# Attention on one core: a tile's six inverse row sums, turned by one transpose, spread over a head's partitions through DRAM, and multiplied on GpSimd

## The chip, the core and the metric

The kernel runs on one core of a Trainium2 chip. The metric is device time in microseconds (us) of one execution; lower is better. The engines are called by the short names of the profile: PE is TensorE (PEld its weight loads), DVE is VectorE, ACT is ScalarE, POOL is GpSimd, and SP is SyncE, which here issues the DMAs.

## The reference, cut to what matters

```
mask   = q_bucket[:, :, :, None] == k_bucket[:, :, None, :]     # hash of 6 sign bits
scores = np.where(mask, scale * q @ k.T, -1e9)
scores = scores - max(scores, axis=-1)
attn   = np.exp(scores)
attn   = attn / (np.sum(attn, axis=-1, keepdims=True) + 1e-9)
x      = attn @ v             # 2 x 8 heads, 768 x 768 scores, head size 64
x      -> [1536, 512] -> a gated MLP (silu) -> a second MLP with softmax and layer norm
```

The change touches one thing: the division of a head's output by its row sums.

## The kernel before, in words

Attention works on eight pairs of heads (a batch and two heads j = 0, 1). A pair's 768 query rows are cut into two halves n of 384 rows. A "quarter" h is one head of one half, three tiles of 128 query rows; there are 32 quarters, numbered in the order of the work, and the quarters with j = 1 close a half: `ends(h)` is true for them (h = 2, 3 and then every odd h from 5 to 31). The main loop (L819 to L868) runs one slot per tile of 128 query rows, 96 of them and nine to drain. In a slot `maxima` takes the row maxima on DVE (L563), `transposes` turns the exponentials of two slots ago on PE (L595, L597), `scores` makes the next tile's scores (four matmuls, L553), `highs` and `lows` split the turned tiles on ACT (L606) and DVE (L610), `values` multiplies by v for the quarter five slots back (L631 to L636), and `exps` is the exponential on ACT (L577). In many slots PE also turns four blocks of the next pair's q and k (L475) or makes hashes (L514). l is the number of a slot within a pair's twelve (slot modulo 12).

The output of a quarter comes off PE transposed: 128 partitions are the high and the low part of the 64 columns of v, and the 384 query rows run along a partition. `results(h)` (L671 to L720) is a generator whose steps the main loop calls in later slots. For a closing quarter: step 1 copies the product to `both_of` on ACT (L703), and two DMAs on SP (L704, L705) lay its halves beside those of the other head, so that `xf` and `low` hold both heads, 64 partitions each; step 2, a slot later, is `widen` (L649): `r`, the 6 inverse sums of each of 128 partitions (2 heads x 3 tiles, L645 and L646, DVE), is stretched to 128 x 384 by two multiplications on POOL (L654); step 3 adds `low` to `xf` on POOL (L710); step 4 is `spread` (L660): three PE transposes of 128 x 128 (L665) put the stretched sums into a PSUM bank; step 5 multiplies `xf` by that bank on DVE (L714); step 6 splits the product into `xh` and `xl` on POOL (L717, L720). Steps 4 and 5 fall into slots with l = 2 and l = 8, step 6 into the slot after. `both_of`, whose buffer has the tag "both", and the PSUM bank "pp" have one buffer each; "pp" also holds the turned blocks and the hashes of the next pair. The last two quarters take another way (L687 to L697).

The order of each engine's work in attention is written out by hand: an engine carries out its instructions in the order in which this loop emits them, and SP issues its DMAs in that order as well. `behind` makes POOL's instruction wait for the latest row maxima. Loads of the next pairs are emitted by `splitting` (L787), at l = 9 the one of q (384 KB). After attention come the two MLPs, on the same engines; their first matmuls (L1132) read `xh` and `xl`.

Of the kernel before, what the change touches and what calls it, by code (L numbers as in the profile page):

```python
# [10 lines left out]
F32 = mybir.dt.float32  # L11
# [10 lines left out]
P = 128  # L22
# [49 lines left out]
def hash_attention_then_two_mlps(  # L72
# [16 lines left out]
    nc = tc.nc  # L89
    B, H, S, D = q.shape  # L90
# [5 lines left out]
    HALF = S // 2  # L96
    CH = C // 2
# [20 lines left out]
    at = ctx.enter_context(ExitStack())  # L118
# [40 lines left out]
    idf = e_sides[2][0][:, :P]  # L159
    make_identity(nc, idf)  # L160
    nc.vector.tensor_copy(idr, idf)
    idf = idr.bitcast(F32)
# [25 lines left out]
    up, down, both = slice(0, D), slice(D, P), slice(0, P)  # L188
# [41 lines left out]
    with at:  # L230
        vp = at.enter_context(tc.tile_pool(name="vp", bufs=2))
        ab = at.enter_context(tc.tile_pool(name="ab", bufs=4))
        sm = at.enter_context(tc.tile_pool(name="sm", bufs=4))
        xs = at.enter_context(tc.tile_pool(name="xs", bufs=2))
        ps_s = at.enter_context(tc.tile_pool(name="ps_s", bufs=1, space=PSUM))
        ps_t = at.enter_context(tc.tile_pool(name="ps_t", bufs=2, space=PSUM))
        ps_a = at.enter_context(tc.tile_pool(name="ps_a", bufs=1, space=PSUM))
        ps_p = at.enter_context(tc.tile_pool(name="ps_p", bufs=1, space=PSUM))
# [56 lines left out]
        def behind(work):  # L295

            if bias_of:
                tc.add_manual_dep(
                    work.ins, bias_of[-1].ins.name,
                    mybir.DependencyInfo(  # L300
                        mybir.DependencyClass.Sync, mybir.DependencyReason.DATA
                    ),
                    reason="behind the maxima",
                )
# [193 lines left out]
        def hashes(p, n, apart=True):  # L498
# [30 lines left out]
        s_of, e_of, t_of, eh_of, el_of, av_of, total_of, r_of, rs_of, x_of = (  # L529
            {} for _ in range(10)  # L530
        )
        NQ = NSLOT // CH

        def quarter(h):


            p, l = divmod(h, 4)
            return (p, l // 2, l % 2) if p == 0 else (p, l % 2, l // 2)

        def ends(h):  # L540

            return quarter(h)[1] == 1
# [95 lines left out]
        def sums(h):  # L638
# [7 lines left out]
            nc.vector.reciprocal(r.rearrange("p j c -> p (j c)"), total)  # L646
            r_of[p, n] = r

        def widen(p, n, tag="wide"):  # L649

            r = r_of[p, n]
            wide = xs.tile([P, CH, 2, D], F32, tag=tag, name="wide", bufs=1)
            for j in range(2):
                behind(nc.gpsimd.tensor_mul(  # L654
                    wide[:, :, j, :], one.unsqueeze(2).to_broadcast([P, CH, D]),
                    r[:, j, :].unsqueeze(2).to_broadcast([P, CH, D]),
                ))
            r_of[p, n] = wide

        def spread(p, n):  # L660

            wide = r_of.pop((p, n))
            rs = ps_p.tile([P, 512], F32, tag="pp", name="pp")
            for c in range(CH):
                nc.tensor.transpose(  # L665
                    rs[:, c * P:(c + 1) * P],
                    wide[:, c].rearrange("p j d -> p (j d)"), idf,
                )
            rs_of[p, n] = rs[:, :HALF]

        def results(h):  # L671


            if not 0 <= h < NQ:
                return
            p, j, n = quarter(h)
            b, hp = pairs[p]
            at = slice(j * D, (j + 1) * D)
            av = av_of.pop(h)
            if j == 0:  # L680
                x_of[p, n] = [
                    xs.tile([P, HALF], F32, tag=tag, name=tag, bufs=bufs)
                    for tag, bufs in (("xf", 3), ("low", 2))
                ]
            xf, low = x_of[p, n]
            cols = slice(b * S + n * HALF, b * S + (n + 1) * HALF)
            if h >= NQ - 2:  # L687

                nc.scalar.copy(low[0:D], av[D:P])
                yield  # L690
                nc.vector.tensor_add(xf[at], av[0:D], low[0:D])
                if j == 0:
                    return
                ends_of["DVE"] = nc.vector.tensor_mul(xf, xf, rs_of.pop((p, n)))
                ends_of["ACT"] = nc.scalar.copy(xh[:, hp, cols], xf)
                nc.vector.tensor_sub(xl[:, hp, cols], xf, xh[:, hp, cols].bitcast(F32))
                return  # L697
            if j == 0:
                nc.scalar.copy(xf, av)
                nc.sync.dma_start(low[0:D], xf[D:P])  # L700
                return
            both_of = xs.tile([P, HALF], F32, tag="both", name="both", bufs=1)
            nc.scalar.copy(both_of, av)  # L703
            nc.sync.dma_start(low[D:P], both_of[D:P])  # L704
            nc.sync.dma_start(xf[D:P], both_of[0:D])  # L705
            del x_of[p, n]
            yield
            widen(p, n)
            yield
            behind(nc.gpsimd.tensor_add(xf, xf, low))  # L710
            yield
            spread(p, n)
            yield
            nc.vector.tensor_mul(xf, xf, rs_of.pop((p, n)))  # L714
            yield
            xh3, xf3 = (x.rearrange("p (c d) -> p c d", d=D) for x in (xh[:, hp, cols], xf))
            behind(nc.gpsimd.tensor_mul(  # L717
                xh3, xf3, one.unsqueeze(2).to_broadcast([P, HALF // D, D])
            ))
            behind(nc.gpsimd.tensor_sub(xl[:, hp, cols], xf, xh[:, hp, cols].bitcast(F32)))  # L720
# [87 lines left out]
        with tc.manual_schedule():  # L808
# [10 lines left out]
            for i in range(NSLOT + 9):  # L819
                p, l = divmod(i, SLOTS)  # L820
                h, part = divmod(i - 5, CH)
# [4 lines left out]
                if part == 0:  # L826
                    leaving, done = done, results(h - 1)
                    go(done)
# [20 lines left out]
                if part == 2 and h == NQ - 1:  # L849
                    spread(*quarter(h)[::2])  # L850
# [11 lines left out]
                if part == 2 and h == NQ - 2:  # L862
                    widen(*quarter(NQ - 1)[::2], "both")
# [648 lines left out]
```

## Time and profile before

| | |
|---|---|
| median of 3 runs | 670.59 us (670.3 to 670.74) |
| the profiled execution, its own time | 670.97 us |
| its span, first to last instruction | 669.1 us |
| PE busy | 661.4 us (99%) |
| DVE, ACT, POOL busy | 530.7, 371.5, 215.4 us |
| granted clock of PE | 1.00 |

A span is cut by the view of windows into stretches with the busy time of each engine in them; the chain of waits follows the work that ended last back from the end, at each step to what released it or to the instruction before it on its engine; the timeline lists single instructions. A matmul's duration in the timeline overlaps that of its neighbours; a step of the chain is only the part by which it moved the end.

### The profile page before, as it was taken

What the parts mean: (1) busy time and instruction counts of PE and PEld (TensorE: products, weight loads), DVE (VectorE), ACT (ScalarE), POOL (GpSimd) and SP (SyncE); (2) the same over time, 40 slices, a digit from 0 to 9 for tenths busy, and PEclk for the clock granted to TensorE, in tenths of its full rate; (3) what the DMA queues carried; (4) which work ended last, traced back from release to release, by engine and by line L of the source; (5) the groups of instructions that cost most, each with busy time, mean ns of one, the idle gap of its engine ahead of it and who ended that gap; (6) DMA issues with size and microseconds to landing.
All of it is one profiled execution on the core that took longest, in us unless ns stands there. A gap on an engine that the chain in (4) does not pass through costs nothing.

```text
span 669.1 us, 10300 instructions
## 1 busy us (share of the span) xinstructions
PE 661.4 (99%) x3653; PEld 578.0 (86%) x3653; DVE 530.7 (79%) x912; ACT 371.5 (56%) x754; POOL 215.4 (32%) x247
## 2 busy tenths in 40 slices
PE   8999999999999999999999999999999999999998
PEld 6999999999999988888888888888888888888887
DVE  7888899999999978957877968858974979865781
ACT  7897998989989944644234234224143533342432
POOL 6647666666626330000000000000000575776200
PEclk9999999999999999999999999999999999999999
DMA  6674754746434123351131543213014220212201
GB/s 188 171 191 118 200 147 106 184 123 168 95 93 142 48 64 119 133 189 63 64 125 64 206 171 90 99 64 119 8 63 154 71 92 36 86 69 96 94 17 48
DMA packets 39347, 73.19 MB, mean 109 GB/s; under 512 B 5336, under 2 KB 26904, under 8 KB 38528
## 3 DMA queue, kind: packets, MB, share of 16 engines
q1 hardware_dynamic: 39296, 72.53, 35.8%
q8 instruction: 29, 0.48, 0.3%
q14 instruction: 22, 0.18, 0.1%
HBM read 40.90 MB, written 7.34 MB: 72 GB/s over the span
## 4 chain that ended last, share of the span: by engine, by line
PE 93%; ACT 3%; DMA 1%; DVE 1%; issue 1%; SPq 0%; ACTq 0%; DVEq 0%
PE h L1132 29%; PE s L553 9%; PE h L1262 8%; PE t L597 5%; PE y L1160 5%; PE y L1159 5%; PE y L1158 5%; PE av L632 4%; PE av L636 4%; PE o L1374 3%; PE o L1376 3%; PE o L1375 3%; PE pp L514 2%; PE pp L475 2%; PE t L1355 1%; PE t L595 1%
## 5 line engine op out<-in xcount | busy, mean ns | idle before, releaser
L610 DVE SCALAR_TENSOR_TENSOR el<-t,eh 128x384 fp32r<-128x384 f32 x192 | 97.6, 550 | 19.1 <-ACT eh L606 18.3
L1132 PE MATMUL h<-xh,hi 128*128 128x512 f32 x288 | 112.2, 390 | 0.0
L1132 PE MATMUL h<-xl,hi 128*128 128x512 f32 x288 | 112.1, 389 | 0.0
L1132 PE MATMUL h<-xh,lo 128*128 128x512 f32 x288 | 111.2, 389 | 0.0
L606 ACT CAST eh<-t 128x384 fp32r<-128x384 f32 x192 | 84.7, 499 | 19.3 <-PE t L597 18.8
L1088 POOL TENSOR_TENSOR sf<-yh 128x256 f32<-128x256 f32 x5 | 3.7, 737 | 277.7 <-ACT yh L1173 277.7
L563 DVE TENSOR_REDUCE top<-s 128x1 f32<-128x770 f32 x96 | 90.7, 945 | 1.0 <-PE s L553 0.8
L632 PE MATMUL av<-eh,vs 128*128 128x384 f32 x186 | 64.6, 347 | 0.1
L1132 PEld LDWEIGHTS h<-xh,hi 128*128 128x128 f32 x288 | 54.1, 188 | 11.3 <-DVE sg L1142 0.2
L1132 PEld LDWEIGHTS h<-xl,hi 128*128 128x128 f32 x288 | 54.1, 188 | 11.2
L1132 PEld LDWEIGHTS h<-xh,lo 128*128 128x128 f32 x288 | 54.0, 188 | 11.2
L1142 DVE TENSOR_TENSOR sg<-h,sg 128x512 f32<-128x512 f32 x36 | 24.8, 689 | 43.3 <-PE h L1132 24.0
L553 PE MATMUL s<-ka,qa 128*128 128x384 f32 x192 | 55.1, 368 | 1.4 <-ACT e1f L577 1.2
L1061 ACT CAST hi<-wf 128x1024 fp32r<-128x1024 f32 x17 | 17.9, 1051 | 68.8 <-DVE wf L68 56.8
L1158 PE MATMUL y<-ah,hi 128*128 128x512 f32 x144 | 56.0, 389 | 0.0
L1159 PE MATMUL y<-al,hi 128*128 128x512 f32 x144 | 56.0, 389 | 0.0
L1160 PE MATMUL y<-ah,lo 128*128 128x512 f32 x144 | 56.0, 389 | 0.0
L1144 ACT CAST ah<-sg 128x512 fp32r<-128x512 f32 x36 | 22.4, 622 | 60.0 <-DVE sg L1142 60.0
L636 PE MATMUL av<-el,vs 128*128 128x384 f32 x155 | 52.3, 337 | 0.0
L553 PE MATMUL s<-kb,qb 76*128 76x384 f32 x192 | 49.4, 338 | 0.0
L1170 DVE TENSOR_TENSOR yf<-y,yf 128x512 f32<-128x512 f32 x60 | 40.2, 684 | 4.8 <-PE y L1160 4.5
L632 PEld LDWEIGHTS av<-eh,vs 128*128 128x128 f32 x186 | 35.0, 188 | 0.4 <-ACT both L703 0.4
(295 smaller groups left out, 1612.1 us busy)
## 6 DMA issues: line engine op xcount, KB each, us to landing
raw<-in_moe_w_out_dram SPq DMA_DIRECT2D x10, 1024.0 KB
raw<-in_moe_w_gate_dram SPq DMA_DIRECT2D x12, 512.0 KB
raw<-in_moe_w_val_dram SPq DMA_DIRECT2D x12, 512.0 KB
ka<-kt SPq DMA_DIRECT2D x30, 192.0 KB
raw<-in_moe_w_in_dram SPq DMA_DIRECT2D x4, 1024.0 KB
parked<-raw SPq DMA_DIRECT2D x8, 512.0 KB
moved<-u SPq DMA_DIRECT2D x8, 512.0 KB
v<-in_v_dram SPq DMA_DIRECT2D x8, 384.0 KB
```

Source lines behind the costliest of these rows:

```text
L553: nc.tensor.matmul(s[:, n, :HALF], a[:, rows], m[:, n * HALF:(n + 1) * HALF], start=first, stop=not first,)
L563: bias_of[:] = [nc.vector.tensor_reduce(tops[i % len(tops)], s_of[i][:, :, :HALF + 1], AX.XY, ALU.max, negate=True)]
L606: nc.scalar.copy(half_tile(eh_of, i, g), t_of[i, g])
L610: last_of[i] = nc.vector.scalar_tensor_tensor(half_tile(el_of, i, g), t_of.pop((i, g)), EVEN, half_tile(eh_of, i, g).bitcast(F32), ALU.add ...
L632: nc.tensor.matmul(av, vj[:, c], eh_of[h][:, c, :], start=c == 0, stop=c == C - 1)
L636: nc.tensor.matmul(*low, start=False, stop=False)
L1132: nc.tensor.matmul(ps[n], a[:, n, kk, :], x[:, kk, blk * BLK:(blk + 1) * BLK], start=kk == 0 and a is hi and x is xh, stop=kk == KD - 1 an ...
L1158: nc.tensor.matmul(p, hi[:, cols], ah, start=f == t * FT, stop=False)
L1159: nc.tensor.matmul(p, hi[:, cols], al, start=False, stop=False)
L1160: nc.tensor.matmul(p, lo[:, cols], ah, start=False, stop=f == (t + 1) * FT - 1)
L1170: nc.vector.tensor_add(y, p, y)
L1262: nc.tensor.matmul(dst, a[m](d), w3_of[b][:, l, d], start=start and n == 0, stop=n == 3 * KH - 1, skip_group_check=True,)
```

## The change

Quarters 5, 7, ... 29 (`kept`, 13 of the 16 that close a half) take another way. Two quarters' results earlier, in step 4 of quarter h - 2, `turn_sums(h)` turns the 128 x 6 inverse sums by one PE transpose into six rows of 128, and DVE copies them from PSUM into `rows`, which takes the buffer "both". In step 6 of quarter h - 2 `keep(h)` writes the six rows to a DRAM tile as two rows of 384, one per head. In step 2 of quarter h `spaced` reads each of the two rows into 64 partitions by a DMA. Step 4 has no `spread`, and step 5 multiplies on POOL. `widen`, `spread` and the DVE multiplication stay for quarters 2, 3 and 31.

```diff
+        rd = at.enter_context(
+            tc.tile_pool(name="rd", bufs=2, space=bass.MemoryType.DRAM)
+        )
...
+        def kept(h):
+
+            return 3 < h < NQ - 1 and ends(h)
+
+        def turn_sums(h, t):
+
+            p, _, n = quarter(h)
+            t = t[:2 * CH, HALF:]
+            nc.tensor.transpose(t, r_of[p, n].rearrange("p j c -> p (j c)"), idf)
+            rows = xs.tile([P, HALF], F32, tag="both", name="rows", bufs=1)[:2 * CH, :P]
+            nc.vector.tensor_copy(rows, t)
+            r_of[p, n] = rows
+
+        def keep(h):
+
+            p, _, n = quarter(h)
+            stored = rd.tile([2, HALF], F32, tag="kept", name="kept")
+            nc.sync.dma_start(stored.rearrange("j (c q) -> (j c) q", c=CH), r_of[p, n])
+            r_of[p, n] = stored
+
+        def spaced(p, n):
+
+            stored = r_of.pop((p, n))
+            wide = xs.tile([P, HALF], F32, tag="wide", name="spaced", bufs=1)
+            for j in range(2):
+                nc.sync.dma_start(
+                    wide[j * D:(j + 1) * D], stored[j:j + 1].to_broadcast([D, HALF])
+                )
+            rs_of[p, n] = wide
...
-            widen(p, n)
+            (spaced if kept(h) else widen)(p, n)
             yield
             behind(nc.gpsimd.tensor_add(xf, xf, low))
             yield
-            spread(p, n)
-            yield
-            nc.vector.tensor_mul(xf, xf, rs_of.pop((p, n)))
-            yield
+            t = None
+            if not kept(h):
+                t = spread(p, n)
+            if kept(h + 2):
+                if t is None:
+                    t = ps_p.tile([P, 512], F32, tag="pp", name="pp")
+                turn_sums(h + 2, t)
+            yield
+            if kept(h):
+                behind(nc.gpsimd.tensor_mul(xf, xf, rs_of.pop((p, n))))
+            else:
+                nc.vector.tensor_mul(xf, xf, rs_of.pop((p, n)))
+            yield
+            if kept(h + 2):
+                keep(h + 2)
```

## Rows read from the trace of the kernel before

**Rows 1.** The page, parts 1 and 2: busy us, and the granted clock by slices.

```profile
PE 661.4 (99%) x3653; PEld 578.0 (86%) x3653; DVE 530.7 (79%) x912; ACT 371.5 (56%) x754; POOL 215.4 (32%) x247
...
PEclk9999999999999999999999999999999999999999
```

**Rows 2.** Windows: length, busy us of PE, PEld, DVE, ACT, POOL, clock, DMA.

```profile
140.00:180.00 40.00, 40.00 (x303) 39.21 (x302) 37.45 (x69) 35.94 (x87) 26.16 (x23) 1.00 0.44 108
```

**Rows 3.** The chain of waits from 60 to 200 us, shares by line.

```profile
by line: PE s L553 29.9%; PE t L597 18.7%; PE av L632 15.2%; PE av L636 12.6%; PE pp L475 8.4%; PE pp L514 7.5%; PE t L595 2.9%; PE av L631 2.5%; PE pp L665 2.4%; issue 0.0%
```

**Rows 4.** The same chain, pieces of one slot with a spread (start, us).

```profile
157.19 0.13 PE t L595
...
158.08 0.33 PE pp L665 x3
...
159.11 0.47 PE t L597 x6
```

**Rows 5.** The tile `wide`: ns least, median, most; first and last start.

```profile
L665 PE MATMUL pp<-idr,wide x48: 270/272/273, 50.5 to 245.5; 128*128 128x128 f32 x48
L654 POOL TENSOR_TENSOR wide<-one,r x32: 503/507/1482, 45.7 to 237.0; 128x192 f32<-128x192 f32 x32
```

**Rows 6.** The tile `xf`, the multiplication and the addition.

```profile
L710 POOL TENSOR_TENSOR xf<-xf,low x15: 1005/1016/1025, 50.5 to 234.3; 128x384 f32<-128x384 f32 x15
L714 DVE TENSOR_TENSOR xf<-xf,pp x15: 535/545/546, 52.2 to 242.4; 128x384 f32<-128x384 f32 x15
```

**Rows 7.** Line 646: the reciprocal of the 128 x 6 sums.

```profile
L646 DVE RECIPROCAL r<-total x16: 177/191/194, 33.1 to 235.9; 128x6 f32<-128x6 f32 x16
```

**Rows 8.** Windows of single slots, l = 2 and l = 0.

```profile
157.12:159.73 2.61, 2.61 (x24) 2.54 (x23) 2.26 (x5) 2.34 (x6) 2.21 (x2) 1.00 0.97 226
152.82:155.15 2.33, 2.33 (x22) 2.29 (x20) 2.29 (x6) 2.33 (x7) 0.97 (x2) 1.00 0.93 251
```

**Rows 9.** Waits of PEld from 60 to 230 us: total, times, longest.

```profile
PEld t L597 <- DVE el L610: 1.7, 6, 0.9
```

**Rows 10.** Line 308: issue times of a DMA from few partitions.

```profile
L308 SPq DMA_DIRECT2D qb<-bits x15: 714/786/1242, 16.6 to 201.0; - x15
```

**Rows 11.** Timeline, SP's issues in five places.

```profile
43.89 0.60 SPq L705 DMA_DIRECT2D xf<-both  x1
...
118.84 0.54 SPq L258 DMA_DIRECT2D q<-in_q_dram  x1
...
160.73 0.46 SPq L308 DMA_DIRECT2D qb<-qa  x1
...
232.08 0.54 SPq L705 DMA_DIRECT2D xf<-both  x1
...
666.40 0.33 SPq L1379 DMA_DIRECT2D out_dram<-ob  x1
```

**Rows 12.** Timeline, ACT's copies to `both` in three places.

```profile
50.42 0.48 ACT L703 COPY both<-av 128x384 f32<-128x384 f32 x1 [1.08 <-DMA xf<-both]
...
121.90 0.51 ACT L703 COPY both<-av 128x384 f32<-128x384 f32 x1
...
163.85 0.48 ACT L703 COPY both<-av 128x384 f32<-128x384 f32 x1 [0.17 <-PE av L632]
```

**Rows 13.** Waits of SP over the span: the last output.

```profile
SPq L1507 <- DMA out_dram<-ob: 1.3, 1, 1.3
```

**Rows 14.** Timeline, POOL at the end of attention.

```profile
234.35 1.01 POOL L710 TENSOR_TENSOR xf<-xf,low 128x384 f32<-128x384 f32 x1 [1.63 <-DMA xf<-both]
236.22 2.29 POOL L654 TENSOR_TENSOR wide<-one,r 128x192 f32<-128x192 f32 x2 [0.86 <-DVE r L646]
243.04 0.83 POOL L717 TENSOR_TENSOR xh<-xf,one 128x384 fp32r<-128x384 f32 x1 [4.52 <-DVE xf L714]
```

**Rows 15.** Timeline, PE: a hash that reads `qb`, and the MLP's matmul.

```profile
164.51 0.33 PE L514 MATMUL pp<-qb,hash_low 128*128 128x384 f32 x1
...
245.48 0.48 PE L1132 MATMUL h<-xh,hi 128*128 128x512 f32 x1
```

More of the change, by code (lines that the diff above doesn't have):

```diff
@@ L669, in spread @@
             rs_of[p, n] = rs[:, :HALF]
+            return rs
         def results(h):
```

## The prediction

> **What bounds the kernel now.** I read the page first, then windows, then the chain, each for a narrower question. The page has PE busy for 99% of the span, at the full one of its two clock levels throughout [rows 1]; so time is bought from PE, but matmul records overlap, and busy is not proof. The window of 40 us in mid-attention has PE without a gap, DVE at 37.45 and ACT at 35.94 us: two engines close behind, POOL at 26.16 with room [rows 2]. The chain decides it: from 60 to 200 us it consists of PE lines alone, and the three transposes of `spread` (L665) are 2.4% of it [rows 3]. That is 3.4 us over the ten spreads of those 140 us. In a slot with a spread the three move the end by 0.33 us [rows 4]. So what PE no longer does there should come off the end nearly in full, as long as DVE and ACT, and the new DMAs, keep up.
>
> **PE.** Thirteen heads' halves (h = 5 to 29) lose their spread: 13 x 0.33 = 4.29 us of chain. Thirteen `turn_sums` come in, one fp32 transpose each: twelve in place of a spread that goes, one in the slot of h = 3, which keeps its own. The six columns of `r` are the operand that is loaded; the 128 columns of the identity stream through as before. I take a third of 0.33, that is 0.11 us. The ends: 0.08, a sixth of the 0.47 us of L597's six, and 0.13, a single fp32 transpose in the chain [rows 4]. So 13 x 0.11 = 1.43 come back, and PE saves 2.86 us (2.6 to 3.25).
>
> A transpose's record lasts 272 ns [rows 5], more than double its step in the chain, because the next one starts under it; a saving is counted in steps. The Trainium skill (TensorE: Matmul & The Clock Gate, Part 4: PE-mode transpose) gives about 275 ns for a 128 x 128 transpose in a kernel's context. The record agrees; as a price it would give 26 x 0.275 = 7.2 us, against 2.86 by the chain.
>
> **DVE.** Thirteen multiplications of 0.545 us go [rows 6]; thirteen copies of 6 x 128 from PSUM come, between 0.19 (the reciprocal of 128 x 6) [rows 7] and 0.545. Scaling the 384 columns down to 128, with some fixed time left, I take 0.28, so 3.4 us less work on DVE. PE waited for DVE only 1.7 us in 170 [rows 9], so I count nothing for it and keep up to 0.3 us for the low end. The copy needs `both_of`'s two DMAs to have landed, three slots after their issue; the bank "pp" comes free sooner than now. Nothing there is late.
>
> Is DVE or ACT next in line? In the slot with a spread PE has 2.61, DVE 2.26, ACT 2.34 us [rows 8]. With 0.22 off, PE has 2.39 and is still the longest, with only 0.05 over ACT. Close, and so a rival below.
>
> **POOL.** Two multiplications of 0.507 go [rows 5], and one of 128 x 384 in the place of the DVE one comes, by the addition of the same shape 1.016 us [rows 6]: no change in sum. It stands later, after the splitting of the next k or q, and `xh`, `xl` are queued behind it, then the splits of the next pair. POOL is idle a third of the time [rows 2] and the splits are used slots later, so this costs nothing; if POOL were full, it would be about 1 us per half. At the end it even helps: for h = 29 `xh` started only at 243.04, behind the DVE multiplication, and the MLP's matmul that reads it at 245.48. The new one can follow POOL's `widen` of 236.22 + 2.29 = 238.5 [rows 14, 15], so `xh` is done over two us earlier, even if the multiplication takes as long as those two halves, 2.29. Hidden.
>
> **DMAs and SP.** Per half three issues: `keep`, up to 0.79 us like the DMA from 12 partitions [rows 10], and two of about 0.5. SP mostly waits for producers, so 1.8 us each six slots (about 14 us) is covered. The reads of 192 KB go into a DMA system that in the slots from l = 0 to l = 2 is 0.93 to 0.97 busy at 226 to 251 GB/s [rows 8]: 0.8 us more of backlog for what follows. The first to be wanted is `qb<-qa`: issued at 160.73, read by the hash at 164.51 [rows 11, 15]. A 96 KB move that POOL waited for took 234.35 - 232.08 = 2.27 us [rows 11, 14]; another 96 KB at 240 GB/s (0.4) and 0.8 of backlog still leave 0.3 us. Cost nothing; at worst, with twice that backlog, 0.5 at each of six places. The reads themselves are wanted two slots after issue, by POOL, which can wait.
>
> **The new wait is `keep`.** `rows` takes the buffer of `both_of`, so ACT's next copy to `both_of` (L703), two slots on, waits until `keep` has landed. ACT's casts are queued behind that copy; DVE, and PE's next transposes, wait for those, and `values` waits for the copy itself. The room: at l = 3 `keep` follows `qb<-qa` (160.73 + 0.46) and the copy stands at 163.85, which leaves 2.66 us. At l = 9 `keep` follows the load of q (118.84 + 0.54) and the copy stands at 121.90, 2.52 us, and 0.22 less once l = 8 is shorter: 2.30 [rows 11, 12]. The first kind stands five times (pairs 2 to 6); the second three times (pairs 2 to 4; pair 1 has more room, and from pair 5 no q is left to load). How long does `keep` take? Alone: the last output, 128 KB to DRAM, is awaited for 1.3 us after an issue of 0.33 [rows 11, 13], so some 1.7; the 96 KB move 2.27. That fits at l = 3. At l = 9, 384 KB of q stand ahead, at some 240 GB/s 1.6 us, of which 0.54 have passed: up to 1.06 more. So 1.7 to 3.3; I take the middle, 2.5, which is 0.2 late, 0.6 us over the three. The ends are 0 and 3 us. A far row is worse: at 43.89 a move under the opening loads held that copy until 50.42, 6.5 us, with ACT idle for 1.08 [rows 11, 12]; none of the new ones meets such a queue.
>
> The Trainium skill (DMA: Bandwidth & Descriptors, Anatomy of one DMA) puts about 2 us of fixed cost on a DMA, described there for another issuing path, mostly the receipt of the write, and heaviest for DRAM. By 2 us alone nothing would be late, and the sum would be 0.6 us better.
>
> **The sum.** 670.97 (the profiled execution) - 2.86 + 0.6 = 668.71. The median stands 0.38 below that execution, so 668.3 us for the median. About 0.2% (1.34 us) is what a measurement of this kernel can tell from no change.
>
> **Rivals.**
> 1. Slower: `keep` lands late at all eight tight places. It pays back the gain at 2.86/8 = 0.36 us late on the mean, and is measurably slower from (2.86 + 1.34)/8 = 0.53. With 3.3 us everywhere it is 3 x 1.0 + 5 x 0.64 = 6.2, so 670.59 - 2.86 + 6.2 = 673.9. For it: room of 2.3 to 2.66 against a nearest row of 2.27, and ACT has little slack. Against it: `keep` is 3 KB, and at l = 3 nothing large is ahead. Chance 0.11.
> 2. PE is relieved, but ACT or the loop of PE, ACT and DVE sets the slot: half of the 0.22 is kept. 670.59 - 1.4 + 0.6 = 669.8. For it: the 0.05 us over ACT. Against: L665 stands in the chain whole, and the slots before and after have other limits. Chance 0.13.
> 3. The chain's steps undercount, and a transpose costs what its record lasts: 670.59 - 26 x 0.272 = 663.5. Against it: L665's three fill 0.49 us of timeline only by overlap, and the next slots are full without a gap. Chance 0.04.
>
> **How the numbers follow.** The forecast has 0.72. Its own ends: low, 670.59 - 3.25 with the 0.3 of DVE waits, 667.0; high, three late `keep`s, 668.3 + 2.4 = 670.7. Rival 2 lies inside. Range 667.0 to 670.7; left out are rivals 1 and 3 and little more. Faster by over 0.2% means under 669.25: most of the forecast (0.66), a little of rival 2 (0.03) and rival 3 (0.04), 0.73. The same: 0.06 of the forecast, 0.10 of rival 2, 0.03 of rival 1, 0.19. Slower: the rest of rival 1, 0.08.
>
> **What would show it.** Right: the chain of a slot with l = 2 or 8 has one transpose of about 0.11 us where three stood, the slot shrinks from 2.61 to about 2.39, and the others keep their length; the copies L703 at l = 5 do not wait, and those at l = 11 of pairs 2 to 4 wait a few tenths for a DMA of `kept<-rows`. Wrong: waits of ACT for that DMA at l = 5 (rival 1); ACT or DVE in the chain at l = 2 and 8 (rival 2); POOL's multiplication waiting for `spaced` so long that splits come late, or PE waiting for `qb` at l = 5, which would show 0.8 us of backlog as too little.

## The result, and the profile after

| | before | after |
|---|---|---|
| median of 6 runs | 670.47 us (670.06 to 671.05) | 675.5 us (674.7 to 677.77) |
| ratio | | 1.0077 [1.0063, 1.009] |
| the profiled execution, its own time | 670.97 us | 675.21 us |
| its span | 669.1 us | 673.2 us |

The change costs 5.0 us where a gain of 2.3 was forecast, and the time lies 4.8 us above the top of the range. The numbers in brackets behind a ratio are its 95% interval. Most line numbers have moved: `scores` L553 is now L556, `maxima` L566, `exps` L580, L597 is L600, `highs` and `lows` L609 and L613, the hash L517, the copy to `both` L703 is L737, the addition on POOL L710 is L744, `xh` and `xl` are L762 and L765, `spread` is L698, the MLP's matmul L1177; of the new lines, L660 is the turn, L662 the copy to `rows`, L669 `keep`, L677 `spaced` and L755 the multiplication on POOL.

The page of the changed kernel, parts 1 and 2, against [rows 1]:

```profile
PE 663.4 (99%) x3627; PEld 576.6 (86%) x3627; DVE 527.0 (78%) x912; ACT 371.9 (55%) x754; POOL 217.7 (32%) x234
...
PEclk9999999999999999999999999999999999999999
```

The clock is the same. DVE has 3.7 us less work, as the sum had it (3.4), and yet the end comes later. So it is not the amount of work, and the slots are read one by one. A slot here runs from the first matmul of one `scores` to that of the next. The chain of waits in a slot with l = 8, where a turn stands for a spread, against [rows 4] (start, us):

```profile
174.11 0.69 PE s L556 x4
174.80 0.11 PE pp L660
174.92 0.17 PE av L635
```

One step of 0.11 us where 0.33 stood: the middle value of the forecast. DVE's copy (line 662: ns least, median, most) took 269 ns, where 280 were taken:

```profile
L662 DVE COPY rows<-pp x13: 269/269/269, 62.0 to 229.5; 6x128 f32<-6x128 f32 x13
```

Windows of four slots of the changed kernel, and under them the same slots of the kernel before (length; busy us of PE, PEld, DVE, ACT, POOL; clock; DMA): l = 8 of pair 5, l = 11 of pair 4, l = 5 of pair 7, l = 0 of pair 6.

```profile
173.86:176.26 2.40, 2.40 (x23) 2.27 (x21) 2.21 (x5) 2.36 (x7) 1.72 (x1) 1.00 0.12 22
152.39:155.15 2.76, 2.75 (x22) 2.30 (x20) 1.78 (x4) 2.68 (x7) 2.19 (x2) 1.00 0.92 218
221.26:223.98 2.72, 2.52 (x17) 1.83 (x16) 1.76 (x4) 2.22 (x6) 0.00 (x0) 1.00 0.15 36
183.04:186.06 3.02, 2.70 (x22) 2.24 (x20) 2.99 (x7) 2.67 (x7) 0.02 (x1) 1.00 0.89 231
```

```profile
171.38:173.98 2.60, 2.60 (x24) 2.53 (x23) 2.42 (x5) 2.33 (x6) 1.85 (x1) 1.00 0.15 28
150.54:152.82 2.28, 2.28 (x22) 2.25 (x20) 1.81 (x4) 2.28 (x7) 1.85 (x1) 1.00 0.98 208
219.18:221.17 1.99, 1.99 (x18) 1.93 (x16) 1.75 (x4) 1.99 (x6) 0.00 (x0) 1.00 0.24 62
180.78:183.38 2.60, 2.58 (x22) 2.25 (x20) 2.57 (x7) 2.60 (x7) 0.97 (x2) 1.00 0.92 245
```

The first is 0.20 us shorter, as forecast. The other three are 0.48, 0.73 and 0.42 longer, and the forecast had 0.2, nothing and nothing for them. The view of waits of the changed kernel from 20 to 270 us (total, times, longest) names two for the new DMAs:

```profile
POOL xf L755 <- DMA spaced<-kept: 2.2, 2, 1.5
ACT both L737 <- DMA kept<-rows: 2.1, 4, 0.8
```

The same view has PE waiting for `qb<-qa` at a hash (0.8 us for the weight load, 0.5 for the matmul), but that place is l = 5 of pair 1, ahead of the first turn, and the kernel before waits 0.4 us there.

ACT waits 2.1 us for `kept<-rows`, in four places (l = 5 of pair 2, l = 11 of pairs 2 to 4). There is a fifth: in the timeline of ACT, the copy at 221.76 (l = 5 of pair 7) is put down to a PE line that had long been done.

```profile
95.74 0.48 ACT L737 COPY both<-av 128x384 f32<-128x384 f32 x1 [0.45 <-DMA kept<-rows]
...
221.76 0.48 ACT L737 COPY both<-av 128x384 f32<-128x384 f32 x1 [0.73 <-PE t L598]
```

What it waits for is seen in SP's issues ahead of it:

```profile
213.05 0.41 SPq L998 DMA_DIRECT2D raw<-in_moe_w_gate_dram  x1
213.51 0.49 SPq L998 DMA_DIRECT2D raw<-in_moe_w_val_dram  x1
214.05 0.50 SPq L1006 DMA_DIRECT2D raw<-in_moe_w_out_dram  x1
215.64 0.48 SPq L734 DMA_DIRECT2D low<-xf  x1
217.26 0.28 SPq L669 DMA_DIRECT2D kept<-rows  x1
```

Two MB of MLP weights are issued from 213.05 on, and `keep` behind them at 217.26. `rows` holds the buffer of `both`; the copy starts 4.50 us after that issue. By the DMA records (the last completion on the DMA's semaphore) `keep` had landed 4.43 us after it. In all five places the copy starts 0.07 to 0.15 us after that landing. So do the copies at l = 5 of pairs 3 and 4 (0.15 and 0.07 us), which the view puts down to PE as well; their slots are 0.14 and 0.13 us longer. That makes seven places.

At the end of attention POOL does what the forecast said: `xh` of h = 29 starts at 242.59, which is 5.7 us after the addition; it was 8.7 in the kernel before [rows 14].

```profile
236.91 1.02 POOL L744 TENSOR_TENSOR xf<-xf,low 128x384 f32<-128x384 f32 x1 [4.24 <-DMA xf<-both]
238.79 2.31 POOL L687 TENSOR_TENSOR wide<-one,r 128x192 f32<-128x192 f32 x2 [0.85 <-issue]
241.06 1.46 POOL L755 TENSOR_TENSOR xf<-xf,spaced 128x384 f32<-128x384 f32 x1
242.59 1.70 POOL L762 TENSOR_TENSOR xh<-xf,one 128x384 fp32r<-128x384 f32 x1
```

But PE's order was changed by it. The order of the MLP's matmuls among the last `values` is not written by hand; a planner sets it when the kernel is built. Now eight matmuls of the MLP stand ahead of the last quarter's `values` that stood behind them before. That the earlier `xh` moved them fits the kernels of the next section: the eight stand ahead in own_rows too, where `xh` is as early, and behind in dve_mul, where it is not. ACT's copy of that quarter (L723), a table load of 1.28 us and the first silu wait behind them, and PE then waits for the silu. ACT's and PE's timeline of the changed kernel:

```profile
244.72 0.48 ACT L723 COPY low<-av 64x384 f32<-64x384 f32 x1
249.49 0.48 ACT L723 COPY low<-t 64x384 f32<-64x384 f32 x1 [4.30 <-PE t L635]
249.98 1.28 ACT L1184 ACT_TABLE_LOAD   x1
251.28 0.60 ACT L1184 ACTIVATE sg<-h 128x512 f32<-128x512 f32 x1
```

```profile
251.93 0.50 PE L1177 MATMUL h<-xh,hi 128*128 128x512 f32 x1 [0.53 <-ACT sg L1184]
```

Between the two copies lie 4.77 us. In the kernel before it is 4.00:

```profile
241.44 0.48 ACT L689 COPY low<-av 64x384 f32<-64x384 f32 x1
245.44 0.48 ACT L689 COPY low<-t 64x384 f32<-64x384 f32 x1 [3.52 <-PE t L632]
```

With both traces cut into slots, the difference after - before (us; starts of slots subtracted, grouped by l and pair; the last columns are kernels of the next section) comes to:

| slots | after | old_tail | own_rows | own_tail | own_tail_conv | q_late |
|---|---|---|---|---|---|---|
| up to the first turn (the same program) | +1.18 | -0.41 | +0.09 | -1.31 | -1.29 | -0.58 |
| twelve with l = 2, 8 that lose a spread | -2.36 | -2.39 | -2.53 | -2.57 | -2.49 | -2.27 |
| h = 3's, a turn beside its spread | +0.20 | +0.20 | +0.25 | +0.26 | +0.25 | +0.20 |
| l = 11, pairs 2 to 4 | +1.49 | +1.59 | -0.04 | -0.06 | -0.02 | -0.05 |
| l = 4 and 5, pairs 2 to 6 | +0.67 | +0.80 | +0.16 | -0.04 | +0.32 | +3.00 |
| l = 5, pair 7 | +0.73 | +2.08 | 0.00 | 0.00 | 0.00 | +0.52 |
| l = 0, pairs 3 to 6 | +0.28 | +0.28 | +1.66 | +1.67 | -0.73 | +1.67 |
| other slots of attention | +0.33 | +0.25 | -0.05 | -0.15 | +0.38 | +0.02 |
| end of attention, the MLPs | +1.54 | -0.29 | +1.49 | -0.32 | -0.29 | +1.52 |

The first row is not the change: those slots come before anything of it runs, and they differ by up to 2.5 us between profiled executions, mostly in one slot (l = 5 of pair 1, from 3.4 to 4.7 us) and at the start. So columns are read from the second row down.

### The profile page after: what moved, and what is told of

It is laid out like the page before. It is cut to its first block, busy times and chain, and to the rows that moved or that the text cites. A ratio compares the mean times of both kernels' runs of the same rounds, so it can differ in the third digit from the quotient of the medians.

```text
span 673.2 us, 10344 instructions
## 1 busy us (share of the span) xinstructions
PE 663.4 (99%) x3627; PEld 576.6 (86%) x3627; DVE 527.0 (78%) x912; ACT 371.9 (55%) x754; POOL 217.7 (32%) x234
## 4 chain that ended last, share of the span: by engine, by line
PE 91%; ACT 3%; DVE 3%; DMA 2%; issue 1%; SPq 0%; DVEq 0%; ACTq 0%
PE h L1177 28%; PE s L556 8%; PE h L1307 8%; PE t L600 5%; PE y L1204 5%; PE y L1203 5%; PE y L1205 5%; PE av L635 4%; PE av L639 4%; PE o L1419 3%; PE o L1421 3%; PE o L1420 3%; PE pp L517 2%; PE pp L478 2%; PE t L1400 1%; PE t L598 1%
## 5 line engine op out<-in xcount | busy, mean ns | idle before, releaser
L613 DVE SCALAR_TENSOR_TENSOR el<-t,eh 128x384 fp32r<-128x384 f32 x192 | 97.5, 548 | 23.8 <-ACT eh L609 22.9
L1177 PE MATMUL h<-xh,hi 128*128 128x512 f32 x288 | 112.3, 390 | 1.2 <-DVE sg L1187 0.7
L1177 PE MATMUL h<-xl,hi 128*128 128x512 f32 x288 | 112.1, 389 | 0.0
L1177 PE MATMUL h<-xh,lo 128*128 128x512 f32 x288 | 111.2, 390 | 0.0
L609 ACT CAST eh<-t 128x384 fp32r<-128x384 f32 x192 | 84.5, 496 | 16.6 <-PE t L600 15.2
L566 DVE TENSOR_REDUCE top<-s 128x1 f32<-128x770 f32 x96 | 90.4, 942 | 1.5 <-PE s L556 1.3
L1177 PEld LDWEIGHTS h<-xh,hi 128*128 128x128 f32 x288 | 54.1, 188 | 13.3 <-DVE sg L1187 1.1
L1177 PEld LDWEIGHTS h<-xl,hi 128*128 128x128 f32 x288 | 54.1, 188 | 11.3 <-DVE xl L730 0.2
L1177 PEld LDWEIGHTS h<-xh,lo 128*128 128x128 f32 x288 | 54.1, 188 | 11.1
L556 PE MATMUL s<-ka,qa 128*128 128x384 f32 x192 | 55.4, 370 | 1.2 <-ACT e1f L580 1.2
L556 PE MATMUL s<-kb,qb 76*128 76x384 f32 x192 | 49.3, 338 | 0.0
```

The source lines that it names most:

```text
L556: nc.tensor.matmul(s[:, n, :HALF], a[:, rows], m[:, n * HALF:(n + 1) * HALF], start=first, stop=not first,)
L566: bias_of[:] = [nc.vector.tensor_reduce(tops[i % len(tops)], s_of[i][:, :, :HALF + 1], AX.XY, ALU.max, negate=True)]
L609: nc.scalar.copy(half_tile(eh_of, i, g), t_of[i, g])
L613: last_of[i] = nc.vector.scalar_tensor_tensor(half_tile(el_of, i, g), t_of.pop((i, g)), EVEN, half_tile(eh_of, i, g).bitcast(F32), ALU.add ...
L1177: nc.tensor.matmul(ps[n], a[:, n, kk, :], x[:, kk, blk * BLK:(blk + 1) * BLK], start=kk == 0 and a is hi and x is xh, stop=kk == KD - 1 an ...
```

## Experiments

Each ratio is against runs of the kernel before on the same chip, whose median was 669.61, 669.91 and 669.95 us in the three groups; the changed kernel's ratio to hold them against is 1.0077.

**own_rows**: `rows` in a buffer of its own. To make room for it, `xf` has two buffers instead of three.

```diff
-            rows = xs.tile([P, HALF], F32, tag="both", name="rows", bufs=1)[:2 * CH, :P]
+            rows = xs.tile([P, P], F32, tag="rows", name="rows", bufs=2)[:2 * CH]
...
-                    for tag, bufs in (("xf", 3), ("low", 2))
+                    for tag, bufs in (("xf", 2), ("low", 2))
```

> The rows get buffers of their own (two of 128 x 128; xf gives up one of its three), so that ACT's copy to both no longer waits for kept<-rows. Theory of the buffer: in the changed kernel the slots behind such a wait are longer (l = 11 of pairs 2 to 4 by 0.48 to 0.52 us each, l = 5 of pair 2 by 0.26, l = 5 of pair 7 by 0.73), so 2.4 us come back: 675.5 - 2.4 = 673.1, and no wait of L737 for a DMA is left. Rival, traffic: ACT's wait only stands in front of a delay that the DMA reads cause in any case; then under 0.5 us come back, 675.0 to 675.5.

Measured: 671.74 us, 1.0032 [1.0019, 1.0044], a gain of 3.0 us over the changed kernel (the difference of the two ratios, 0.0045, of 670). The waits at l = 11 and at l = 5 are gone, all of them (table). But the four slots at l = 0 are 1.66 us longer now. Windows of own_rows (columns as above): l = 11 of pair 4, l = 5 of pair 7, l = 0 of pair 6.

```profile
150.58:152.85 2.27, 2.27 (x21) 2.23 (x20) 1.83 (x3) 2.27 (x7) 2.19 (x2) 1.00 0.96 208
220.96:222.90 1.94, 1.94 (x18) 1.90 (x16) 1.91 (x6) 1.67 (x5) 0.00 (x0) 1.00 0.36 73
180.74:183.74 3.00, 2.68 (x21) 2.22 (x20) 2.96 (x7) 2.66 (x7) 0.00 (x0) 1.00 0.91 240
```

**old_tail**: PE's order at the end of attention as it was: in the MLP's first step, the tenth matmul of the second block, and with it all that follow, is put behind the last `spread`.

```diff
+                    if f == 0 and blk == 1 and m == 9:
+                        late.enter_context(tc.issue_after(last_of["PE"].ins))
```

(`last_of["PE"]` is the transpose in `spread`, kept there by one more assignment.)

> The changed kernel with PE's order at the end of attention as before: the MLP's 34th matmul and what follows it wait in PE's order behind the last quarter's values and spread. Theory of the order: the planner put eight MLP matmuls ahead of the last quarter's values, so ACT's last copy, the table load and the silu behind it came later; from the 34th matmul to the 85th the kernel lost 1.5 us, which come back: 674.0, with the MLP's 85th matmul no later against the kernel before than the first. Rival: the loss there comes from POOL's late xh and xl of quarter 29 or from DVE's conversions, whatever PE's order is: 675.0 to 675.8.

Measured: 672.88 us, 1.0051 [1.0039, 1.0064], 1.7 us below the changed kernel. The chain of waits from 236 to 262 us, changed kernel first, then old_tail:

```profile
by line: PE h L1177 39.8%; DVE lo L1012 9.4%; ACT L1184 4.9%; DVE wf L68 4.8%; DVE wf L60 4.8%; ACT hi L1106 4.1%; PE t L635 4.1%; DVE sg L1187 4.0%; PE t L639 3.4%; PE av L635 2.7%; issue 2.7%; DVE wf L58 2.7%; DVE wf L56 2.6%; ACT sg L118
```

```profile
by line: PE h L1180 84.5%; PE t L635 4.0%; PE t L639 3.4%; PE av L635 2.7%; PE av L639 2.0%; PE t L600 1.5%; PE pp L698 1.3%; PE av L634 0.7%; PE t L634 0.7%; PE t L598 0.5%
```

In the changed kernel PE's matmuls hold 40% of that chain; the rest is DVE and ACT working one after the other on what came late. With the old order PE's lines make nearly all of it, and the second copy (old_tail, ACT's timeline) stands 2.94 us behind the first:

```profile
244.58 0.48 ACT L723 COPY low<-av 64x384 f32<-64x384 f32 x1
247.52 0.48 ACT L723 COPY low<-t 64x384 f32<-64x384 f32 x1 [2.46 <-PE t L635]
```

So the order costs 1.8 us (+1.54 against -0.29). The 0.3 us that the end gains with the old order is not the earlier `xh`: dve_mul, below, gains as much there, and its `xh` starts 8.7 us after the addition (248.05 and 239.36), as in the kernel before. What both lack is the spread of h = 29, 0.33 us of chain.

**no_reads**: the two DMAs of `spaced` are left out; POOL multiplies by ones, so that 13 halves stay undivided.

```diff
-            wide = xs.tile([P, HALF], F32, tag="wide", name="spaced", bufs=1)
-            for j in range(2):
-                nc.sync.dma_start(
-                    wide[j * D:(j + 1) * D], stored[j:j + 1].to_broadcast([D, HALF])
-                )
-            rs_of[p, n] = wide
+            rs_of[p, n] = one.to_broadcast([P, HALF])
```

> The DMA reads of the stored sums are left out; POOL multiplies by a column of ones in their place, so the 13 halves stay undivided. The write of the rows and its buffer stay. Theory of traffic: the reads (2.5 MB, 192 KB per half, in slots in which the DMA system is over 0.9 busy) hold up qb<-qa, for which PE waits 1.4 us at the hashes, and keep; so 1.4 to 2 us come back, 673.5 to 674.1. Theory of the buffer alone: keep follows the load of q in any case, so the 0.5 us at l = 11 of pairs 2 to 4 stay, and only the hashes' part (0.9 us of slot lengths) comes back. Rival: the reads are hidden, 675.2 to 675.8.

Measured: 674.3 us, 1.0072 [1.0058, 1.0085], which can't be told from the changed kernel. The slots with l = 5 of pairs 2 to 6 are no longer than in the kernel before, where the changed kernel had added 0.58 us: `keep` of l = 3 lands 2.09 to 2.14 us after its issue here, 2.10 to 2.80 in the changed kernel, and no copy at l = 5 of those pairs waits for it. So the reads cost something there, by way of `keep`. But the waits for `keep` grew in the other places (l = 11: +2.19, l = 5 of pair 7: +2.22), and the time as a whole separates nothing as long as those waits are there; best_noreads, below, does. The waits at the hashes of which the expectation speaks are those of pair 1.

**dve_mul**: the multiplication on DVE again, by the tile that the DMAs filled.

```diff
-                behind(nc.gpsimd.tensor_mul(xf, xf, rs_of.pop((p, n))))
+                nc.vector.tensor_mul(xf, xf, rs_of.pop((p, n)))
```

> The multiplication of the 13 halves goes back from POOL to DVE, from the spaced sums in SBUF; all else as changed. With it the planner puts the eight MLP matmuls back behind the last quarter's values. Theory of the order: the 1.5 us of the tail come back, and attention stays as it is, with DVE paying 0.55 us in slots where PE has 2.4: 674.0. Rival, POOL: its multiplication holds up DVE in attention (the conversion L68 took 1.43 us against 1.00 before, a slot of 3.02 us against 2.60), then more, 673.4. Rival, DVE: it becomes the limit in slots l = 2 and 8, up to 0.2 us in each of 13: 675 to 676.6.

Measured: 675.15 us, 1.0081 [1.0067, 1.0095]; the rival had it. PE's old order at the end comes back by itself (-0.33 there), yet slots with l = 9 are 0.7 us longer in pairs 2 to 5, and those with l = 3 by 0.2 to 0.9. DVE then carries the copy and the multiplication one behind the other, and the multiplication waits for POOL. dve_mul, POOL and DVE:

```profile
174.58 1.85 POOL L276 TENSOR_TENSOR qs<-q,qs 128x768 fp32r<-128x768 f32 x1 [1.62 <-DVE top L566]
```

```profile
175.76 1.09 DVE L755 TENSOR_TENSOR xf<-xf,spaced 128x384 f32<-128x384 f32 x1
```

It takes 1.09 us here and 0.54 in the median; it ends 0.42 us after POOL's subtraction. The four of l = 8 in pairs 2 to 5, which lie beside such a subtraction, take 1.08 or 1.09 us each.

**What stands at l = 0.** The same can be seen in own_rows. A step of the conversion of MLP weights falls into l = 11 and l = 0 on DVE; line 68 in pairs 4 and 6, line 58 in pairs 3 and 5. POOL and then DVE, in the kernel before and in own_rows:

```profile
178.52 1.85 POOL L273 TENSOR_TENSOR vs<-v,vs 128x768 fp32r<-128x768 f32 x1 [0.39 <-DVE top L563]
```

```profile
179.91 1.00 DVE L68 CUSTOM_DVE_ANT_0 w1f<-raw,w1f 128x1024 uint16<-128x1024 uint16 x1
```

```profile
178.88 1.86 POOL L276 TENSOR_TENSOR vs<-v,vs 128x768 fp32r<-128x768 f32 x1
```

```profile
179.87 1.42 DVE L68 CUSTOM_DVE_ANT_0 w1f<-raw,w1f 128x1024 uint16<-128x1024 uint16 x1
181.21 0.95 DVE L566 TENSOR_REDUCE top<-s 128x1 f32<-128x770 f32 x1
```

In the kernel before the conversion ends 0.55 us after POOL's subtraction (180.91 and 180.37); in own_rows too (181.29 and 180.74). Over before, after and own_rows, line 68 starts 0.97 to 1.51 us after the start of POOL's subtraction and always ends 0.54 or 0.55 us behind it; line 58 always ends 0.28 us behind. It gets done when POOL is done, whenever it started. POOL's queue now holds the multiplication of 1.01 us ahead of `xh`, `xl` and this split of v, and the subtraction ends 0.37 us later. In the changed kernel it is the 0.42 of the windows in pair 6; in pairs 3 to 5 it doesn't show, where ACT's wait at l = 11 comes just ahead and holds back what DVE does before the conversion. The Trainium skill (SBUF — State Buffer, SBUF: two separate sides) describes one pair of ports that GpSimd and certain VectorE operations share, locked for a whole instruction. The 0.55 us in these traces agree.

**own_tail** is own_rows and old_tail together.

> The change with rows of their own and with PE's old order at the end of attention, both at once. If they are two separate losses, their gains add: rows of their own stand at +2.1 us against the kernel before (1.0032), the old order took 1.0077 - 1.0051 of the change's time, 1.7 us; together about +0.4 us, ratio 1.0006. The MLP's first matmul then starts as in own_rows (0.4 to 0.5 us ahead of before) and the end keeps that, where own_rows gave back 1.5 us behind it. Rival: what the old order gains is only the room that the wait at l=5 of pair 7 left; without that wait it gains nothing, ratio 1.002 to 1.003. What is left in attention is 0.41 us at l=0 of pairs 3 to 6, each.

Measured: 669.9 us, 1.0 [0.9989, 1.001]. The two gains add; the rival's 1.002 is outside the interval. What is left is the l = 0 slots, +1.67.

**own_tail_conv**: own_tail, with the conversion's third step of a pair moved to the next pair's l = 0.

```diff
-                if p > 1 and l in (3, 9, 11):
+                if (p > 1 and l in (3, 9)) or (p > 2 and l == 0):
                     go(first_weights)
```

> As own_tail, and the step of the MLP weights' conversion that DVE does at l=11 moved to l=0 of the next pair, where POOL is idle from 180.74 to 184.35 us in own_rows. Lock theory: DVE's conversion cannot run while POOL's subtraction of v's low parts does (in three traces it ends 0.55 us behind it, whenever it started); POOL's multiplication makes that subtraction end 0.37 us later. Then the record of 1.42 us falls to about 0.55, the slots with l=0 of pairs 3 to 6 lose 0.41 us each and more (down to the 2.3 us of the others), and the time comes to -1.3 us or below against the kernel before, ratio 0.998 or less. Rival: the slots at l=0 are long for another reason (transfers, the order of the tile program); the conversion keeps its 1.0 to 1.4 us or the slots don't shorten, ratio 1.0006 as own_tail.

Measured: 668.18 us, 0.9972 [0.9962, 0.9983]. POOL and DVE:

```profile
176.31 1.86 POOL L276 TENSOR_TENSOR vs<-v,vs 128x768 fp32r<-128x768 f32 x1
181.38 1.02 POOL L744 TENSOR_TENSOR xf<-xf,low 128x384 f32<-128x384 f32 x1 [3.22 <-DMA qb<-qa]
```

```profile
179.73 0.65 DVE L68 CUSTOM_DVE_ANT_0 w1f<-raw,w1f 128x1024 uint16<-128x1024 uint16 x1
```

POOL is idle from 178.17 to 181.38, and the conversion takes 0.65 us instead of 1.42. The l = 0 slots go from +1.67 to -0.73.

**before_conv**: the same move in the kernel before, alone.

> The kernel before with the same step moved alone, so that a gain of the move isn't put down to the change. Lock theory: here POOL spreads the sums (two of 0.97 us) just where the step now falls, so it waits there instead of at the subtraction; its records stay at 1.0 us or over in the four places, and the time is that of before or up to 1 us more, ratio 1.000 to 1.0015. Rival: the later place is better by itself, whatever POOL does: 0.3 to 0.4 us gained at two or more places, ratio 0.9985 to 0.999.

Measured: 669.31 us, 0.999 [0.9981, 0.9999]: the rival had it, and my expectation was wrong about the place: 0.97 us is the time of both multiplications of `widen`, not of each, and they are over when the step starts. Line 68 takes 0.65 us here too, against 1.00 in the kernel before, and the l = 0 slots are 0.72 shorter. So the lock cost the kernel before as well. Of the 1.9 us by which own_tail_conv beats the kernel before (0.0028 x 669.9), 0.7 are the move's and 1.2 the change's (by the two intervals, give or take 0.9): own_tail_conv to before_conv is 0.9972/0.999 = 0.998.

**best_noreads** is own_tail_conv with the edit of no_reads; the 13 halves stay undivided again.

> own_tail_conv without the 26 reads that spread the rows over a head's partitions; POOL multiplies by ones, so 13 halves stay undivided. If the reads cost nothing of their own (they wait for nobody, and their traffic delays no transfer that anybody waits for), the time is that of own_tail_conv within 0.4 us. If their share of the DMA engines delays the hash reads, it is 0.5 us or more below own_tail_conv, and the slots with l=5 shorten.

Measured: 667.87 us, 0.9975 [0.9963, 0.9986], as own_tail_conv. Here, where nobody waits for `keep`, the 26 reads cost nothing that can be measured.

**xf_two**: the other half of own_rows' edit alone, two buffers of `xf`.

> The changed kernel with two buffers of xf instead of three and nothing else: the part of own_rows that only made room for its tile. If own_rows gained because its rows no longer share the buffer of `both`, this one gains nothing: ratio 1.0077 as the changed kernel, within 0.001, and the slots with l=11 of pairs 2 to 4 stay 0.5 us longer than before. Rival: the two buffers of xf are what shifted the waits; then the time is nearer to own_rows, 1.003 to 1.005.

Measured: 674.66 us, 1.0075 [1.0056, 1.0094]; l = 11 is +1.55. The gain of own_rows is its own buffer's.

**q_late**: the load of q, which is 384 KB (the expectation has the size wrong), behind `keep` instead of just ahead of it.

```diff
-            loads = {6: ((p + 3, "k"),), 9: ((p + 3, "q"),), 0: ((p + 1, "v"),)}
+            loads = {6: ((p + 3, "k"),), 11: ((p + 3, "q"),), 0: ((p + 1, "v"),)}
```

> The changed kernel with the load of q moved from l=9 to l=11, so that the store of the six rows is no longer issued 0.63 us behind a load of 768 KB. If that load is why the store of l=9 lands after 2.66 to 2.79 us (pairs 2 to 4) and not after about 2.1, it lands 0.5 us sooner or more, ACT no longer waits for it at l=11, and three slots lose 0.5 us each: 1.5 us off the changed kernel, ratio 1.0055. The slots with l=5 (0.1 to 0.3 us at pairs 2 to 5, 0.7 at pair 7) keep what they lost. Rival: the store itself or the small moves ahead of it take that long; it lands after 2.6 us still, ratio 1.0077.

Measured: 676.56 us, 1.0086 [1.007, 1.0101]. By the DMA records in the trace `keep` of l = 9 landed 1.64 to 1.66 us after its issue instead of 2.66 to 2.79, and at l = 11 nobody waits: the mechanism was right. The time was not, because the load is now ahead of other things. It stands just ahead of the load of v and of the moves of l = 0 to 3; `keep` of l = 3 lands after 2.74 to 3.10 us in pairs 2 to 5 (2.12 to 2.80 in the changed kernel), and in pair 2 it is issued 1.5 us later in its slot. Which of the things ahead held it up is not shown. Three copies to `both` of q_late (pair 2: l = 5, then l = 11; pair 4: l = 5), and the waits from 70 to 140 us:

```profile
81.19 0.48 ACT L737 COPY both<-av 128x384 f32<-128x384 f32 x1 [2.59 <-DMA kept<-rows]
...
95.17 0.51 ACT L737 COPY both<-av 128x384 f32<-128x384 f32 x1
...
138.16 0.48 ACT L737 COPY both<-av 128x384 f32<-128x384 f32 x1 [1.17 <-PE t L598]
```

```profile
PEld pp L517 <- DMA qb<-qa: 1.4, 1, 1.4
...
PE pp L517 <- DMA qb<-qa: 1.1, 1, 1.1
```

The copy of l = 5 in pair 2 waits 2.59 us. Just ahead of it one hash waits for `qb`, its weight load 1.4 us and its matmul 1.1 of the same time. With l = 11 free, the l = 0 slots show their +1.67.

## Why the prediction was wrong

**PE.** Right. Thirteen spreads' steps went, a turn costs 0.11; twelve slots gave 2.3 to 2.6 us back, h = 3's took 0.2, the end of attention gave 0.3 once the old order was restored. That is -2.5 against -2.86. Rivals 2 and 3 fall with it: eleven of the twelve slots are 0.20 to 0.23 us shorter in the changed kernel, and the twelfth (l = 2 of pair 5, only 0.04 there) is 0.23 shorter in own_rows.

**"The new wait is `keep`."** The mechanism was right, two of its terms were mis-sized. At l = 11 the lateness is 0.5 us, not 0.2: `keep` landed after 2.66 to 2.79 us in pairs 2 to 4, not 2.5, and 1.49 us were lost instead of 0.6. The sentence that failed outright is "none of the new ones meets such a queue": the weights' loads of the MLPs are issued in pair 7, I had counted the tight places by the loads of q alone, and `keep` landed after 4.43 us there. That place took 0.73 us in the profile of the changed kernel, 0.52 in q_late and 1.44 to 2.22 in old_tail, no_reads, dve_mul and xf_two, where `rows` still has the buffer of `both`. At l = 5 of pair 2 ACT waited 0.81 us for it, and the slot grew by 0.26; the forecast had put `keep` there at 1.7 to 2.27 us, within the room of 2.66, and it took 2.80. With own_rows all of it goes, 3.0 us as timed, with the 1.4 us that the l = 0 slots took on already subtracted. So rival 1's mechanism took place at six of its eight places (l = 11 of pairs 2 to 4, l = 5 of pairs 2 to 4), and at one that it did not count.

**"POOL ... costs nothing."** False, in a way that no sum of busy time shows. POOL's sum is unchanged (217.7 us, 215.4 before), and nobody waits for its result. But the conversion on DVE does not get done while POOL's subtraction runs beside it, so POOL's *position* is a cost: 0.28 us in the changed kernel, 1.66 when the waits that covered it were gone.

**"At the end it even helps ... Hidden."** Half right: `xh` is early. But its earliness moved the planner's order of PE, and that order cost 1.8 us, while no run shows a gain from the earlier `xh`. The step that is missing is what a planner does with an instruction that can start earlier.

**"DMAs and SP ... cost nothing."** Right where `rows` has its own buffer, by best_noreads against own_tail_conv, and in own_rows the slots with l = 5 of pairs 2 to 6 are 0.03 us longer in sum. In the changed kernel the reads made `keep` late at l = 5, up to 0.58 us by no_reads. No hash of pairs 2 to 6 waits for `qb` in the changed kernel.

The steps of the sum as they turned out, in the profile of the changed kernel: -2.4 + 0.2 (spreads), +1.5 (l = 11), +0.7 (l = 4 and 5), +0.7 (pair 7), +0.3 (l = 0), +0.3 (other slots), +1.5 (end) = +2.8 us. The timed difference is 5.0. Pair 7's wait was small in that execution, which may be up to 1.5 us of it. The rest stays open: in eight of the ten kernels run here, too, the timed difference lies 0.7 to 1.5 us above that of their slots. A part of it lies outside the span from the first to the last instruction: an execution takes 1.8 to 1.9 us more than its span in the kernel before (medians), and 2.1 to 2.7 in those eight. What fills it no run shows. It also isn't known why l = 10 of pair 6 is 0.4 to 0.5 us longer in every kernel in which POOL multiplies (-0.09 in dve_mul), with 0.26 of it given back at l = 9.

## What to carry to other kernels

A new tile that takes an old tile's buffer makes the old tile's writer wait for the slowest transfer of the new one: look at what is in the DMA queues at every place where it stands, not at the usual one, and price the buffer first. Where engines are packed, a moved instruction costs by what stands beside it and by what a planner then reorders; compare the orders of all engines before and after, and look for records of another engine that change their length with it. When several covers lie over each other, one repair shows the next loss (own_rows at l = 0, q_late at l = 5), so repairs are tried together as well as alone.

## What the runs showed of the hardware that was not expected

The conversion on DVE of line 68 takes 0.65 us with POOL idle and up to 1.43 beside a POOL subtraction, ending 0.55 us behind it in each of the traces of before, after and own_rows; line 58 takes 0.38 and up to 1.17. A store of 3 KB to DRAM landed, by the DMA records, after 1.2 us for the last half, 1.6 ahead of a load of 384 KB (q_late), 2.7 to 2.8 behind one (after) and 3.9 to 5.9 behind 2 MB of weights (all kernels with `keep`): what stands ahead of it moved its time, at the same size.
